# A linear-attention and mixture-of-experts kernel on one core: the first ten steps of the pipeline in a written-out order

## The chip, the cores and the metric

The kernel runs on one core of a Trainium2 chip. The metric is the device time of one execution, in microseconds (us). A core has five instruction streams that run side by side [...]: PE (TensorE, the matrix multiplies; PEld is its weight load), ACT (ScalarE), DVE (VectorE), POOL (GpSimd) and SP (SyncE, which here issues nearly all loads). Each stream executes its own instructions strictly in the order in which the program lists them.

## What is computed

The first half is a gated linear attention over 4 batches, 8 heads, 768 tokens and a head width of 48:

```
f = sigmoid(f_logit)
for t in range(S):
    state = f[t, :, None] * state + outer(k[t], v[t])
    y[t]  = q[t] @ state
```

The second half sends each of the 3072 rows (384 wide: 8 heads by 48) to one of 8 experts. The reference is

```
logits = x @ w_gate;  e = argmax(logits);  gate = softmax(logits)[e]
out[row] = gate * (relu(x[row] @ w1[e]) @ w2[e])        # w1: 384 x 1024, w2: 1024 x 384
```

All of it is in 32-bit floats.

## The kernel before

**Units and steps.** The attention is cut into chunks of 128 tokens. One *unit* is one chunk of two batches, so there are 12 units (NU = 12), each of 8 head pairs, which stand as two *halves* `a` and `b` of four pairs. Units `u` and `u+2` follow each other in time for the same two batches; their state passes from one to the other. What one unit needs, with the function and the line (of the kernel before) that the profile shows, and the engine:

- `load` (SP, L485): f, k, q, v of a unit from memory, each into the next of 2 (f), 3 (k), 4 (q) or 3 (v) buffers.
- `steps` (ACT, L495) and `log` (ACT, L503): exp and ln of the gate; `total` (DVE, L510): the running sum of the logs; `growth` (ACT, L524): r = exp(sum); `decay` (ACT, L539): exp(-sum), over the gate's own buffer.
- `by_r` (POOL L528, for some units DVE L528): k times r, in place; `by_decay` (DVE, L551): q times the decay, in place. `ends` and `last_decay` (POOL, L534 and L546) copy the last column of the sum and of the decay.
- `score` (PE, L562): k against q into four PSUM banks; `mask` (DVE, L568): four predicated copies, half `a` first, into `at`.
- `keys` (PE, L577): the scaled k transposed; `keep` (ACT, L582): copied to `kn`.
- `within` (PE, L590): v against the masked scores into `yt`; `before` (PE, L611): the old state against q, added to `yt`; `settle` (ACT, L652): `yt` copied to `ys`.
- `added` (PE, L627): `kn` against v, the state's increment `dp`; `update` (DVE L642 for units 0 and 1, L644 later; then POOL, L646): new state.
- `rows` (PE, L682): `ys` times the gate matrix and a selection matrix, which brings the tokens onto partitions; then the logits' reduction (DVE, L690); `lay` (ACT, L707 and L712): the rows copied to `xr`.
- For each two units one `Route`: `choose` (DVE, L228 to L236), `count` (PE, L240 and L241), `weigh` (ACT, L268), `place` and `fill` (DVE, L247 to L274), and `send` (POOL, L195): indirect DMAs that put each row into its expert's region.

**PSUM.** Scores have four banks, `yt` has two (one tile for both halves), and the transposed keys, `dp` and the rows' result share the last two: `turns` gives these tiles in alternation to two banks, so each waits until the tile two before it has been read out.

**What sets the order.** The pool's scheduler is switched off (`manual_schedule`): each engine's stream is the order in which the Python code calls the functions. A first block (L716 to L822) handles the start: loads, 24 filler multiplies into `yt` (`warm`, L729), units 0 and 1 by halves, 8 more fillers. Then comes the loop `for n in range(1, NU + 2)`: step n scores unit n (`here`), works `within` and `before` on n-1 (`back`), makes the rows of n-2 (`last`), and runs the gates of n+1 to n+3 ahead. Cases for n of 1, 2 and 3 put the pieces of the first steps in other places of the step. From step 10 on no gates are left but a rest of unit 11's.

**After the loop** the eight experts are worked: `widen` (L336, two matrix products with a 1024-wide hidden layer, ReLU at L346 on ACT and L348 on DVE), `narrow` (L352, the result scaled at L363 on DVE and scattered at L195 on POOL), and for the rows that do not fit an expert's regular blocks the quads (L1121, L1147, L380). The first row blocks of experts 0 and 1 are begun in the loop's last steps (n of 12 and 13).

The functions that the change touches, as they were:

Of the kernel before, what the change touches and what calls it, by code (L numbers as in the profile page):

```python
# [19 lines left out]
C = 128  # L20
# [100 lines left out]
def kernel(  # L121
# [318 lines left out]

    with ExitStack() as st:
# [7 lines left out]
        yt = psy.tile([128, 2, HP, C], F32, name="yt")  # L449
        nc.vector.memset(yt, 0.0)  # L450
# [119 lines left out]
        def keys(u):  # L570
            x = units[u]
            x["kn"] = wk.tile([128, SEG, C], F32, name="kn", bufs=1)
            x["kp"] = []
            for a in range(2):
                kp = turns("kp", [128, HP, C])
                for p in range(HP):
                    nc.tensor.transpose(kp[:, p], x["k"][:, HP * a + p], ident)  # L577
                x["kp"].append(kp)

        def keep(u):  # L580
            for a in range(2):
                nc.scalar.copy(units[u]["kn"][:, HP * a : HP * a + HP], units[u]["kp"][a])  # L582

        def within(u, a):

            x = units[u]
            if a == 0:
                x["yt"] = yt
            for p, h, _ in heads():
                nc.tensor.matmul(  # L590
                    x["yt"][DP * (h ^ a) : DP * (h ^ a) + D, a, p],
                    lhsT=x["v"][:, a, 2 * p + h],
                    rhs=x["at"][:, a, h, p],
                    start=p == 0,
                    stop=x["old"] is None,
                    skip_group_check=True,
                )

        def before(u):
# [6 lines left out]
            for p in range(HP):  # L606
                for h in range(2):
                    for a in range(2):
# [3 lines left out]
                            x["yt"][to : to + D, a, p],  # L612
# [7 lines left out]
        def added(u):  # L620
# [3 lines left out]
            for a in range(2):  # L624
                for p, h, r in heads():
# [3 lines left out]
                        lhsT=x["kn"][:, s, r],  # L629
# [6 lines left out]
        def update(u):  # L636
# [3 lines left out]
            last = _bc(x["last"], 2, D)  # L640
# [5 lines left out]
            return lambda: nc.gpsimd.tensor_tensor(new, new, last, op=OP.mult)  # L646

        def settle(u):
            x = units[u]
            x["ys"] = wk.tile([128, 2, HP, C], F32, name="ys", bufs=1)  # L650
            for a in range(2):
                nc.scalar.copy(x["ys"][:, a], x["yt"][:, a])  # L652
# [10 lines left out]
        def rows(u, counted=None):  # L663
# [11 lines left out]
            x["xr"], x["xp"] = group["xr"][:, 2 * (u - g[0]) :], []  # L675
            for a in range(2):
                j = 2 * (u - g[0]) + a
                xp, counts = pair()
                if a and counted:
                    counted.count(counts[:, :, 0 : counted.n])  # L680
                for p in range(HP):
                    done["rows"] = nc.tensor.matmul(  # L682
                        xp[:, p],
                        lhsT=x["ys"][:, a, p],
                        rhs=wx[:, p, 0:XW] if a else wx[:, p, E:WX],
                        start=True,
                        stop=True,
                    ).ins
                gate = slice(0, E) if a else slice(2 * D, XW)
                nc.vector.reduce_sum(  # L690
                    group["lg"][:, j],
                    xp[:, :, gate].rearrange("p h e -> p e h"),
                    axis=AX_X,
                )
                x["xp"].append(xp)
# [4 lines left out]
        def lay(u):  # L700

            x = units[u]
            for a in range(2):
                to = x["xr"][:, a, 0:DM].rearrange("p (h w) -> p h w", h=HP)
                if a:
                    for h in range(2):
                        nc.scalar.copy(  # L707
                            to[:, :, D * h : D * h + D],
                            x["xp"][a][:, :, XW - D * h - D : XW - D * h],
                        )  # L710
                else:
                    nc.scalar.copy(to, x["xp"][a][:, :, 0 : 2 * D])  # L712
# [4 lines left out]
        load(0, "f", ab)  # L717
        load(0, "k")
        load(1, "f", ab[:1])
        load(0, "q")  # L720
        load(1, "f", ab[1:])
        load_first_consts()
        load(1, "kq")
        for i in (1, 0):
            nc.gpsimd.memset(scores[i], 0.0)
        def warm(count):

            for _ in range(count):
                nc.tensor.matmul(yt[:, 0, 0], lhsT=pad[:, 0:C], rhs=pad[:, 0:C], start=True, stop=True)  # L729

        warm(24)
        for part in ab:
            steps(0, part)
            total(0, part)
        load(2, "f")
        load(0, "v")
        for part in ab:
            growth(0, part)
            by_r(0, part, nc.vector)
            decay(0, part)  # L740
        for part in ab:
            by_decay(0, part)
        ends(0)
        last_decay(0)
        lay_selection()
        for part in ab:
            steps(1, part)
        load(3, "f")
        load(2, "k")
        load(1, "v")  # L750
        load(2, "q")
        load_gate()
# [42 lines left out]
        score(0, 0)  # L795
        score(0, 1)
        keys(0)
        warm(8)
        for part in ab:
            total(1, part)  # L800
        for a, part in enumerate(ab):
            growth(1, part)
            by_r(1, part)
            decay(1, part)
            for h in range(2):
                mask(0, a, h)
            scaled = by_decay(1, part)
            if a == 0:
                routed.append(scaled)
        ends(1)  # L810
        last_decay(1)
        steps(2)
        load(4, "f")
        load(3, "k")
        load(3, "q")
        load(2, "v")
        total(2)
        keep(0)
        steps(3, logs=False)
        growth(2)  # L820
        load(5, "f")
        load_consts()  # L822

        for n in range(1, NU + 2):
            here, back, last = n, n - 1, n - 2
            ahead = n + 1 < NU
            state = n < NU - 2
# [3 lines left out]
            if 2 < last:  # L831
                settle(last)
# [5 lines left out]
            if ahead and not 1 < n < 4:  # L838
# [11 lines left out]
            if n == 1:  # L850
                units[0]["old"] = None
                added(0)
                update(0)()
            if ahead and not 1 < n < 4:
                decay(n + 1)
                last_decay(n + 1)
            if state:
                keys(here)
                keep(here)
            if 1 < n < 4:  # L860
                growth(n + 1)
                if n == 3:
                    by_r(n + 1)
                ends(n + 1)
                decay(n + 1)
                last_decay(n + 1)
            if here < NU:
                for a in range(2):
                    for h in range(2):
                        if n == 2 and a and h:  # L870
                            by_r(n + 1, on=nc.vector)
                        mask(here, a, h)
            if n == 1:
                log(3)
                within(0, 0)
                within(0, 1)
                settle(0)
            if n == 1:
                steps(4, logs=False)
# [488 lines left out]
```

## Time and profile before

| | us |
|---|---|
| runs of the kernel before | 389.91, 390.06, 401.82; median 390.06 |
| the profiled execution's own time | 393.27 |
| span of its instructions, first to last | 391.5 |
| PE / DVE / ACT / POOL busy in the span | 377.9 / 171.0 / 102.8 / 113.7 |
| granted TensorE clock, mean | 0.996 |
| first score starts | 9.94 |
| scores of units 1 to 11 start | 15.04, 23.88, 32.26, 41.95, 52.48, 61.95, 71.33, 80.57, 89.95, 99.16, 106.46 |
| first multiply of the experts (L336) | 119.47 |

The span lies inside the time of the execution, 393.27 - 391.5 = 1.8 us around it. "Busy" counts each engine by itself, so the shares do not add up. PE's ends are modelled: two neighbouring groups of multiplies overlap by some 0.07 us in the list, and a group that holds a short wait shows as a longer group. In the list in order of time a row is: start, duration, engine, line, operation, output and inputs, count, and in brackets the idle time before it and what ended it. A 32-bit multiply stands as two entries (x16 is eight multiplies).

### The profile page before, as it was taken

What the parts mean: (1) busy time and instruction counts of PE and PEld (TensorE: products, weight loads), DVE (VectorE), ACT (ScalarE), POOL (GpSimd) and SP (SyncE); (2) the same over time, 40 slices, a digit from 0 to 9 for tenths busy, and PEclk for the clock granted to TensorE, in tenths of its full rate; (3) what the DMA queues carried; (4) which work ended last, traced back from release to release, by engine and by line L of the source; (5) the groups of instructions that cost most, each with busy time, mean ns of one, the idle gap of its engine ahead of it and who ended that gap; (6) DMA issues with size and microseconds to landing.
All of it is one profiled execution on the core that took longest, in us unless ns stands there. A gap on an engine that the chain in (4) does not pass through costs nothing.

```text
span 391.5 us, 7712 instructions
## 1 busy us (share of the span) xinstructions
PE 377.9 (97%) x3054; PEld 264.7 (68%) x3054; DVE 171.0 (44%) x366; ACT 102.8 (26%) x190; POOL 113.7 (29%) x120
## 2 busy tenths in 40 slices
PE   7899999999999999999999999999999999999993
PEld 7887888999989678685555555654466466464452
DVE  6998998979663632112121131116413013111450
ACT  7887977775432001010100110000010010001000
POOL 5772688897645310100001001000100100100011
PEclk9999999999999999999999999999999999999998
DMA  7999657778982359694549999898173469992231
GB/s 276 384 396 359 206 200 256 233 223 315 395 295 106 127 157 321 166 322 101 191 123 397 237 399 395 201 401 236 40 260 94 101 233 387 404 407 95 80 122 42
DMA packets 51659, 94.81 MB, mean 242 GB/s; under 512 B 20840, under 2 KB 40875, under 8 KB 49568
## 3 DMA queue, kind: packets, MB, share of 16 engines
q1 hardware_dynamic: 48448, 84.62, 64.0%
q0 software_dynamic: 3168, 9.64, 6.6%
q8 instruction: 25, 0.41, 0.4%
q14 instruction: 18, 0.15, 0.1%
HBM read 79.23 MB, written 15.21 MB: 241 GB/s over the span
## 4 chain that ended last, share of the span: by engine, by line
PE 84%; DVE 8%; issue 2%; DMA 2%; ACT 1%; POOL 1%; SPq 0%; POOLq 0%; DVEq 0%; ACTq 0%
PE hps L336 28%; PE yps L352 24%; PE yps L1147 7%; PE xp L682 5%; PE yt L590 4%; PE s L562 4%; PE s L336 3%; DVE sum L510 3%; PE hps L1121 3%; PE yt L611 2%; PE yp L352 2%; DVE at L568 2%; DMA q<-in_qu_dram 2%; DVE q L551 1%; PE kp L577 1%
## 5 line engine op out<-in xcount | busy, mean ns | idle before, releaser
L336 PE MATMUL hps<-xT,w1t 128*128 128x352 f32 (+2 forms) x384 | 110.1, 447 | 0.0
L336 PEld LDWEIGHTS hps<-xT,w1t 128*128 128x128 f32 x384 | 72.7, 190 | 37.2 <-issue 1.9
L352 PE MATMUL yps<-w2t,hT 128*128 128x384 f32 x288 | 94.4, 487 | 0.0
L195 POOL DMA_INDIRECT out_dram<-ysb,dst x24 | 23.4, 975 | 224.4 <-DVE ysb L363 214.7
L352 PEld LDWEIGHTS yps<-w2t,hT 128*128 128x128 f32 x288 | 54.6, 190 | 38.6 <-issue 1.5
L346 ACT ACTIVATE hT<-hps 128x352 f32<-128x352 f32 (+2 forms) x28 | 13.8, 491 | 200.4 <-PE hps L336 171.7
L348 DVE TENSOR_SCALAR hT<-hps 128x352 f32<-128x352 f32 (+2 forms) x28 | 15.6, 558 | 93.0 <-PE hps L336 93.0
L363 DVE TENSOR_SCALAR ysb<-yps,tg 128x384 f32<-128x384 f32 x22 | 13.6, 618 | 74.4 <-PE yps L352 55.6
L195 POOL DMA_INDIRECT xs<-xr,posi x24 | 32.9, 1371 | 18.7 <-issue 4.3
L568 DVE COPY_PREDICATED at<-mpack,s 128x512 f32<-128x512 uint8 x48 | 31.3, 727 | 4.9 <-PE s L562 4.9
L510 DVE TENSOR_TENSOR_SCAN sum<-g,cap 128x1032 f32<-128x1032 f32 (+1 forms) x14 | 28.9, 2070 | 2.6 <-ACT g L503 2.6
L528 POOL TENSOR_TENSOR k<-k,r 128x1024 f32<-128x1024 f32 (+1 forms) x11 | 24.1, 2190 | 14.1 <-ACT r L524 7.1
L1147 PE MATMUL yps<-qw,hqT 128*32 128x192 f32 (+1 forms) x192 | 27.5, 381 | 0.3 <-issue 0.2
L562 PE MATMUL s<-q,k 64*128 64x128 f32 x384 | 24.9, 279 | 1.8 <-POOL rend L534 1.3
L682 PE MATMUL xp<-wx,ys 128*128 128x104 f32 x192 | 25.2, 281 | 0.9 <-ACT kn L582 0.7
L562 PEld LDWEIGHTS s<-q,k 64*128 64x128 f32 x384 | 22.5, 188 | 3.9 <-issue 1.9
L590 PE MATMUL yt<-at,v 128*48 128x128 f32 x384 | 25.1, 276 | 0.0
L682 PEld LDWEIGHTS xp<-wx,ys 128*128 128x128 f32 x192 | 22.7, 191 | 2.8 <-issue 1.4
L590 PEld LDWEIGHTS yt<-at,v 128*48 128x48 f32 x384 | 20.0, 123 | 2.6 <-issue 1.5
L1147 PE MATMUL yps<-w2t,hT 128*32 128x384 f32 x192 | 21.4, 487 | 0.0
L551 DVE TENSOR_TENSOR q<-q,g 128x1024 f32<-128x1024 f32 (+1 forms) x14 | 16.5, 1188 | 0.3 <-DMA q<-in_qu_dram 0.3
L1147 PEld LDWEIGHTS yps<-w2t,hT 128*32 128x32 f32 x192 | 7.6, 110 | 13.0 <-issue 12.5
(116 smaller groups left out, 362.5 us busy)
## 6 DMA issues: line engine op xcount, KB each, us to landing
qw<-in_moe_w_dram SPq DMA_DIRECT2D x16, 1536.0 KB
w1t<-in_moe_w_dram SPq DMA_DIRECT2D x8, 1536.0 KB
w2t<-in_moe_w_dram SPq DMA_DIRECT2D x8, 1536.0 KB
k<-in_ku_dram SPq DMA_DIRECT2D x12, 512.0 KB
q<-in_qu_dram SPq DMA_DIRECT2D x12, 512.0 KB
f<-in_fu_dram SPq DMA_DIRECT2D x10, 512.0 KB
xs<-pad SPq DMA_DIRECT2D x8, 600.0 KB
v<-in_vu_dram SPq DMA_DIRECT2D x12, 384.0 KB
```

The source lines that it names most:

```text
L195: ins = nc.gpsimd.indirect_dma_start(out=dst, out_offset=bass.IndirectOffsetOnAxis(ap=idx, axis=0), in_=src, in_offset=None, bounds_check= ...
L336: nc.tensor.matmul(x["h"][:, f], lhsT=w[0][:, j, b * 128 : b * 128 + 128], rhs=x["xT"][:, j], start=j == 0, stop=j == KD - 1,)
L348: nc.vector.tensor_scalar(to, x["h"], 0.0, None, op0=OP.max)
L352: nc.tensor.matmul(yp, lhsT=x["hT"][:, f, t * C : t * C + C], rhs=w[1][:, f, :], start=f == 0, stop=f == NF - 1,)
L510: nc.vector.tensor_tensor_scan(x["sum"][:, part].rearrange("p s c -> p (s c)"), x["g"][:, part].rearrange("p s c -> p (s c)"), cap[:, part ...
L528: ins = on.tensor_tensor(k, k, units[u]["r"][:, part], op=OP.mult).ins
L551: return nc.vector.tensor_tensor(q, q, x["dec"][:, part], op=OP.mult).ins
L562: done["score"] = nc.tensor.matmul(ps[h][:, p], lhsT=x["k"][r, s], rhs=x["q"][r, s], start=True, stop=True).ins
L568: nc.vector.copy_predicated(x["at"][:, a, h], _bc(causal, 1, HP), x["ps", a][h])
L590: nc.tensor.matmul(x["yt"][DP * (h ^ a) : DP * (h ^ a) + D, a, p], lhsT=x["v"][:, a, 2 * p + h], rhs=x["at"][:, a, h, p], start=p == 0, st ...
L682: done["rows"] = nc.tensor.matmul(xp[:, p], lhsT=x["ys"][:, a, p], rhs=wx[:, p, 0:XW] if a else wx[:, p, E:WX], start=True, stop=True,).ins
L1147: nc.tensor.matmul(yp[r], lhsT=h[:, f, at : at + T], rhs=w[:, f, cols], start=f == 0, stop=f == NF - 1, skip_group_check=True,)
```

## The change

The code before and at the start of the loop, up to and including step 9, is replaced by one string, FIRST_STEPS, of short pieces. `lf0a` is "load f of unit 0, half a", `sc3b` "score of unit 3, half b", `kp` the transposed keys, `keep` their copy, `wi` within, `bef` before, `dp` added, `upd` and `updp` the two parts of update, `set` settle, `xp` and `lg` and `lay` the rows, their logits and their copy, `mx` and `my` the masks of a half, `exp ln sum r dec` the gates, `kr krx krv` by_r (plain; behind the latest DVE result named; on DVE), `q` by_decay, `oh ex place send` the route, `fill` the fillers. A regular expression reads the string and calls the functions one after the other; since the schedule is manual, each engine's stream is the string's order, filtered. The loop now runs from step 10 to 13 and keeps the order it had for these steps.

Three tiles are split by halves, so that a half can be written while the other is still in use: `kn` (two tiles, one buffer each), `ys` (two tiles) and `yt` (two PSUM tiles of one bank each). Counted on each engine, the instructions are the same before and after by kind and number (PE 1663, ACT 239, POOL 189, SP 467), except that DVE's zeroing of `yt` is two instructions instead of one (454 for 453). SP's stream of loads is the same, load for load.

```diff
+    FIRST = 10
+    FIRST_STEPS = """
+        lf0a exp0a ln0a fill24 lf0b exp0b lk0 ln0b sum0a dec0a sum0b ends0 lf1a lq0 lf1b r0a
+        r0b exp1a krv0a krv0b consts0 kp0a lk1 ln1a q0a sc0a lq1 exp1b ln1b dec0b keep0a
+        sum1a sel0 fill8 dec1a r1a sum1b r1b kr1a q0b q1a kp0b kr1b keep0b lf2 lv0 lf3 lk2
+        lv1 mx0a my0a lq2 sc0b mx0b my0b last0 dp0 upd0 sc1a exp2 ln2 wi0a gate0 lf4 kp1a
+        dec1b lk3 lq3 lv2 kp1b ends1 sum2 ends2 q1b exp3 lf5 wi0b set0a keep1a last1 mx1a
+        sc1b my1a mx1b r2 krx2 consts1 keep1b dp1 my1b wi1a set0b kp2a upd1 kp2b dec2 q2 ln3
+        sum3 ends3 exp4 ln4 upd0p upd1p sc2a mx2a sc2b keep2a keep2b my2a last2 dec3 line0
+        r3 xp0a xp0b set1a lq4 wi1b last3 lg0a lay0a mx2b my2b set1b wi2a wi2b dp2 lg0b krv3
+        bef2 line1 line2 lk4 lv3 lf6 pads0 lk5 lv4 lay0b kp3a exp5 ln5 sum4 r4 q3 exp6 sc3a
+        sc3b upd2 krx4 upd2p kp3b mx3a my3a keep3a xp1a dec4 mx3b my3b keep3b xp1b lg1a q4
+        lg1b last4 lay1a dp3 sum5 lq5 lay1b sc4a sc4b ends4 ends5 oh1 kp4a upd3 lf7 set2a
+        wi3a set2b wi3b mx4a my4a mx4b ln6 kp4b lk6 r5 kr5 dec5 q5 keep4a xp2a lv5 keep4b
+        bef3 exp7 lg2a xp2b lay2a set3a set3b dp4 lq6 lf8 lk7 sum6 sc5a lg2b lay2b my4b
+        ends6 dec6 upd4 ex1 place1 ln7 wi4a q6 sc5b lv6 r6 upd3p kp5a kp5b lq7 last5 last6
+        mx5a kr6 lf9 wi4b lk8 lv7 keep5a line3 xp3a keep5b xp3b my5a sc6a mx5b upd4p my5b
+        sc6b lg3a exp8 ln8 lay3a lg3b lay3b bef4 oh3 lq8 set4a lf10 set4b send5 sum7 r7 krx7
+        dec7 last7 dp5 kp6a sum8 upd5 wi5a ends7 ends8 mx6a my6a mx6b wi5b bef5 kp6b line4
+        lk9 keep6a xp4a keep6b q7 my6b set5a lv8 lq9 ex3 xp4b dec8 lg4a lg4b lay4a sc7a q8
+        wi6a lay4b r8 place3 send6 dp6 upd6 kp7a sc7b mx7a my7a mx7b set5b line5 wi6b keep7a
+        kp7b xp5a my7b krx8 sc8a exp9 ln9 keep7b xp5b exp10 ln10 lg5a sum9 lg5b oh5 lay5a
...
+        bef8 my9a mx9b lg7a lay7a dp9 sum11 r11 lg7b lay7b my9b oh7 upd9
+    """
...
-        yt = psy.tile([128, 2, HP, C], F32, name="yt")
-        nc.vector.memset(yt, 0.0)
+        yt = [psy.tile([128, HP, C], F32, name=f"yt{a}") for a in range(2)]
+        for y in yt:
+            nc.vector.memset(y, 0.0)
...
-            x["kn"] = wk.tile([128, SEG, C], F32, name="kn", bufs=1)
...
+        def keys(u, a):
+            x = units[u]
+            x["kn", a] = wk.tile([128, HP, C], F32, name=f"kn{a}", bufs=1)
+            kp = x["kp", a] = turns("kp", [128, HP, C])
...
-            x["ys"] = wk.tile([128, 2, HP, C], F32, name="ys", bufs=1)
-            for a in range(2):
-                nc.scalar.copy(x["ys"][:, a], x["yt"][:, a])
+            for a in halves:
+                x["ys", a] = wk.tile([128, HP, C], F32, name=f"ys{a}", bufs=1)
+                nc.scalar.copy(x["ys", a], x["yt"][a])
...
+        for what, u, part in re.findall(r"([a-z]+)(\d+)([abp]?)", FIRST_STEPS):
+            DO[what](int(u), part)
...
-        for n in range(1, NU + 2):
+        for n in range(FIRST, NU + 2):
```

## The prediction

> **What bounds the kernel now.** I read the page's first part and its chain first: PE is busy 97% of the span and carries 84% of the chain, so an engine other than PE can only matter where PE stands still. Where that is, the page does not say; the busy times by stretch do. The columns are PE, PEld, DVE, ACT and POOL busy, then granted clock, DMA share, GB/s; the first score starts at 9.94.
>
> ```profile
> 9.94:20.00 10.06, 9.00 (x125) 8.14 (x126) 9.86 (x12) 8.65 (x16) 7.13 (x6) 1.00 1.04 381
> 20.00:30.00 10.00, 9.42 (x142) 8.58 (x143) 9.93 (x12) 8.02 (x13) 7.68 (x8) 1.00 1.02 400
> 30.00:40.00 10.00, 9.21 (x140) 8.08 (x140) 8.18 (x13) 7.98 (x16) 3.23 (x4) 1.00 0.87 328
> 40.00:50.00 10.00, 9.33 (x158) 8.39 (x154) 9.86 (x17) 9.12 (x15) 6.18 (x6) 1.00 0.59 200
> 50.00:60.00 10.00, 9.75 (x170) 8.48 (x166) 9.79 (x19) 7.88 (x16) 8.14 (x8) 1.00 0.59 198
> 60.00:72.00 12.00, 12.00 (x226) 10.70 (x224) 9.89 (x26) 8.80 (x16) 9.12 (x11) 1.00 0.83 266
> ```
>
> From 60 on PE has no idle time (39.20 of 39.20 us up to 99.2). Before that its gaps sum to 3.35 us, beside a DVE that is nearly full in four of five stretches. The chain of waits agrees: to 59.6 it runs over DVE, ACT and POOL, from there over PE alone. One undisturbed step of it gives PE's prices (start, us, what):
>
> ```profile
> 62.02 1.99 PE s L562 x32
> 64.00 1.02 PE kp L577 x8
> 65.03 1.01 PE yt L590 x16
> 66.04 1.07 PE xp L682 x8
> 67.11 0.16 PE xp L240 x2
> 67.27 0.22 PE xp L241 x2
> 67.49 0.95 PE xp L682 x8
> 68.45 1.01 PE yt L590 x16
> 69.46 0.92 PE dp L627 x32
> 70.38 1.02 PE yt L611 x32
> ```
>
> So a unit costs PE: score 1.99, keys 1.02, within 2.02, rows 1.96 (0.38 more in every second unit for the counts), dp 0.92, before 1.02: 9.1 us. The bound to any gain follows. By 59.60 PE has done 6 scores (11.94), 6 keys (6.12), 5 within (10.1), 4 rows with one count (8.2), 5 dp (4.6), 2 before (2.0) and the eight late fillers (1.95): 44.9 us of work in 49.66. Lost: 4.7, of which 3.3 are visible gaps and the rest waits inside groups. The same sum from 59.60 to 99.23 is 38.4 of 39.6: lost 1.2. With the fillers, 7.8 us could be had at the very most, which is just 2% of the time. What follows step 9 isn't touched, and starts as much earlier as PE gets there.
>
> **The change part by part.** *Nothing is removed or added* but one DVE zeroing split in two at the start (0.91 us before in one; the fillers wait 2.1 us on DVE's zeroing either way): 0 on the path, bounded by -0.1 and +0.1. The order of SP's loads is the same; f, k and q of units 0 and 1 wait for nothing computed, so q0 lands at 9.19 as before. Later loads wait for a buffer's last reader: k3 for unit 0's score, which I put 2 to 3 us later below, but f4 ahead of it on SP issues at 16.28 only because exp2 ends then, so k3 keeps its place; behind it lie q3, v2, f5, the second constants, q4, k4, all likewise. The DMA engines are full until 36 either way, and no load is waited for after q0: 0, with +1 if one comes late.
>
> *The order.* I followed each engine's new order by hand: an instruction starts when its engine is free and its inputs are there, at this trace's durations (ACT half 0.54, whole 0.96, exp whole 1.2; DVE half scan 1.27, scan 2.3, mask 0.65, q 0.6 a half and 1.2 whole; POOL half k 1.4, whole 2.37). Unit 0 loses: keys 0a now stand ahead of score 0a, and need the identity, whose arrival ends POOL's wait at 10.25, so score 0a is 10.75 to 11.75 (9.94 before); the fillers run to 13.7; keys 0b, score 0b 14.2 to 15.2; dp0 to 16.1. Score 1a then has what it needs (q1a 13.6, k1a 14.7): 16.1 to 17.1. Before, at 17.1, PE had 4.1 us of work done (fillers aside); after, 4.9. Behind it PE always has a piece whose inputs are there: within 0a, keys 1, within 0b to 20.1, score 1b, and dp1 at 21.5 (its copied key 1b ends then, 0.4 lost), within 1a; keys 2 wait for k2 on POOL (r2 20.95 + 2.37 = 23.4, 0.4 lost); q2 ends at 24.3, and score 2 starts at 24.4.
>
> Next, score 2 to 26.5; rows 0 wait for the bank of keys 2a (copied 26.85, 0.35 lost); within 1b to 29.9; within 2a for settle 1a, which ACT has behind dec3 and r3 (29.9). dp2, before 2, keys 3a to 34.3, when q3 is just done (sum3 26.7, masks, k3 on DVE 30.8, sum4 33.1, q3 34.3). Score 3, keys 3b, rows 1, dp3 to 39.7; q4 39.3; score 4 39.7 to 41.7. Unit 5's score starts at 49.2, unit 7's first half at 66.5, its second ends at 70.9 (before, score 7 starts at 71.39 in the chain). On the way PE ends keys 4a at 42.4, within 3 44.4, keys 4b 44.9, rows 2a 45.9, before 3 46.9, rows 2b 48.3, dp4 49.2, score 5a 50.2, within 4a 51.2, score 5b 52.2, keys 5 53.2, within 4b 54.2, rows 3 56.2, score 6 58.2, before 4 59.2, dp5 60.1, keys 6a 60.6, within 5 62.6, before 5 63.6, keys 6b 64.1, rows 4 66.5, score 7a 67.5, within 6a 68.5, dp6 69.4, keys 7a 69.9. It waits for none of them, since DVE ends q5 at 46.4, the last mask of unit 4 at 49.7, q6 53.0, the last mask of unit 5 at 55.6, unit 5's update 62.6, q7 65.8, and POOL ends k5 at 45.6, k6 55.3, k7 63.7. A check by work done:
>
> | at (after / before) | done after | done before | ahead |
> |---|---|---|---|
> | 24.4 / 23.88 | 11.9 | 9.9 | 2.0 - 0.5 = 1.5 |
> | 41.7 / 41.95 | 28.7 | 26.7 | 2.0 + 0.3 = 2.3 |
> | 53.2 / 52.48 | 40.0 | 36.0 | 4.0 - 0.7 = 3.3 |
> | 70.9 / 71.39 | 57.7 | 54.2 | 3.5 + 0.5 = 4.0 |
>
> The lead comes in two places: PE has keys and within of a unit to do while POOL and DVE finish the next k and q (20 to 34), and rows 2 no longer stand in a gap behind the copied keys (0.67 at 46.7).
>
> *The halves.* Split `kn`, `ys`, `yt` take waits off: within 2a needs settle 1a only. That lies inside the walk. What the walk leaves out is the handoff. The rows of before show it where an input is only just ready:
>
> ```profile
> 35.45 0.66 PE L577 MATMUL kp<-fpack,k 128*128 128x128 f32 x4 [0.55 <-DVE state L644]
> 31.19 1.14 PE L627 MATMUL dp<-v,kn 128*64 128x48 f32 x32 [0.25 <-ACT xr L712]
> 50.40 1.14 PE L627 MATMUL dp<-v,kn 128*64 128x48 f32 x32 [0.19 <-ACT xr L712]
> ```
>
> I take 0.2 for each of the walk's four short waits up to unit 2, about 0.7 in all: 4.0 - 0.7 = 3.3. From both sides: a gain of 4.0 and 0.5 of what is lost after unit 7, or 1.6 less than 3.3 if in eight steps one more bank is handed over late by 0.2.
>
> *The port.* One rule speaks against a tight order: the Trainium skill, "SBUF — State Buffer", section "Who interferes with whom", says that a VectorE instruction with two SBUF inputs and a GpSimd one that reads SBUF exclude each other for the whole instruction. The trace shows the price: q of unit 4 starts at 39.22 during POOL's k (37.76 to 40.13) and takes 1.99 instead of 1.21. The walk has such meetings at q1a (k1 of POOL at 13.35) and q5 (k5 43.2 to 45.6). By the row 0.8 each, by the rule up to 1.4 and 2.4. q1a would end at 15.0 instead of 13.6, under dp0 (to 16.1); q5 at 46.9 instead of 46.4 or, by the rule, 48.8, under before 3, rows 2b and dp4 (to 49.2). Both hide; without that cover they cost 1.6 by the row and 3.8 by the rule. I take 0.
>
> **Sum.** 391.5 - 3.3 = 388.2 of span; with the 1.8 us around it 390.0, against 393.27 for the profiled run. The median of the runs is 390.06, 3.2 below that run, so the time is 390.06 - 3.3 = 386.8.
>
> **The rivals.** *Most of the lead is lost to handoffs.* PE's waits of 0.2 to 0.5 come back at every bank of the two that keys, dp and rows share, now three to five times a step in a new order. Lead 0.5 to 2: 388.0 to 389.6, say 389. For it: DVE at 9.8 of 10 us leaves little for the early copies that free these banks. Against it: from 60 to 106 the same rotation runs without a gap.
>
> *PE is dense from the first score on.* 4.7 + 1.2 lost come back, less 1.3 at the start: gain 4.6 to 6, 384.5. Against it: the walk itself already shows 1.3 us of waits.
>
> *DVE becomes the bound (slower).* Place: units 3 to 9. DVE's step is sum 2.3, q 1.2, masks 2.6, state 0.54, logits 0.35, half a route 1.45: 8.45 against PE's 9.1. If POOL's k, sum ends and last-decay copies meet sum and q in each step, at 0.8 for each of two, a step is 10.05, 0.9 over PE's: seven steps cost 6.3, 386.8 + 6.3 = 393. It decides from 0.7 us of meetings a step, and the gain is gone at 1.2. For it: DVE's 9.86 of 10 between 40 and 50. Against it: 8.1 to 8.4 a step between 60 and 99 with the same work, and POOL's k stand behind a named DVE result in units 2, 4, 7 and 8.
>
> *It does nothing:* the stages before 60 would have to be hidden, but the chain runs straight through them.
>
> **How the numbers follow.** As forecast (gain 2.2 to 4.5, 385.6 to 387.9): 0.58. Handoffs (388 to 389.6): 0.20. Dense (384 to 385.5): 0.11. DVE bound or a late load (390 to 398): 0.11. The range of 8 in 10 leaves a tenth at each end: 384.5 to 390.0. 2%, which is about what a measurement of this kernel can tell from no change, is 7.8 us, all that PE's losses hold: faster by more 0.03; slower by more (over 397.9, DVE at 1.9 us of meetings a step) 0.03; within 0.94.
>
> **What would show it.** Score 0 starting near 10.7, later than before; PE's idle time from there to 60 at about 1.3 instead of 3.35; score 7's second half over at 70.9; the experts' first multiply at 116.2 instead of 119.47; the expert part itself unchanged in length (272.0 from there). Wrong if PE's gaps recur after 60, where DVE would then be full, or if a load is named as a releaser after q0.

## The result, and the profile after

The changed kernel takes 388.42 us (median of 22 runs, 387.05 to 390.20), the kernel before 390.04 beside it; the ratio is 0.9966, 95% interval 0.9954 to 0.9978, a gain of 1.3 us by the ratio (1.6 by the medians) where 3.3 was forecast. Its runs lie in two groups with 0.63 us between them: 13 from 387.05 to 388.60 (middle one 387.70), 9 from 389.23 to 390.20 (middle one 389.79), the latter at a mean granted clock of 0.991 to 0.995 (0.9926 on average), the former at 0.995 to 0.999 (0.9974). Two slow runs of the kernel before, 401.82 and one read as 999.0, stay out of the ratio; its other 20, from 388.96 to 390.68, are one group. The profiled execution took 388.52, its span is 386.5.

The same stretches as in the prediction, now of the kernel after (PE, PEld, DVE, ACT, POOL busy, granted clock, DMA share, GB/s):

```profile
9.94:20.00 10.06, 8.97 (x126) 8.07 (x127) 9.35 (x11) 8.87 (x17) 4.36 (x6) 1.00 1.04 382
20.00:30.00 10.00, 9.92 (x149) 8.80 (x148) 9.60 (x14) 9.72 (x15) 5.25 (x10) 1.00 1.01 365
30.00:40.00 10.00, 9.98 (x186) 9.18 (x183) 9.22 (x14) 8.46 (x15) 3.73 (x7) 1.00 0.93 357
40.00:50.00 10.00, 10.00 (x176) 9.03 (x172) 9.86 (x17) 8.28 (x17) 3.17 (x4) 1.00 0.76 255
50.00:60.00 10.00, 10.00 (x154) 8.96 (x152) 8.46 (x25) 7.13 (x13) 6.13 (x7) 1.00 0.63 235
60.00:72.00 12.00, 12.00 (x215) 10.81 (x208) 11.21 (x23) 8.61 (x16) 8.11 (x9) 1.00 0.70 241
```

The gaps are gone: from 20 to 60 PE stands still for 0.1 us instead of 2.29 (the missing 1.09 of the first row is the time before the first piece, at 11.03). The list of PE's waits up to the experts has four entries left (what waited, for what, us in total, times, longest):

```profile
PE yt L754 <- DVE yt L482: 1.6, 1, 1.6
PE kp L607 <- DMA fpack<-c_fpack: 1.4, 1, 1.4
PE xp L717 <- ACT ys L681: 0.2, 1, 0.2
PE s L337 <- DVE xT L320: 0.2, 1, 0.2
```

The last one was not there before: the experts' first multiply waits for `xT`, the transposed rows. The chain of waits of the kernel after (start, us, what) runs through the rows at that place, where PE carried it alone in the forecast:

```profile
101.98 0.78 POOL state L673
102.77 0.17 issue
102.94 1.84 POOL xs L196
104.77 0.31 issue
105.08 5.77 DMA xs<-xr,posi
...
112.38 4.24 DMA xrow<-xs
...
116.75 0.71 DVE xT L320
117.45 0.04 issue
117.50 2.27 PE s L337 x18
```

The sixth pair of row scatters is issued at 102.94 and 105.08, its last packets land at 110.85, only then SP may read the first expert's rows back, the last of four reads lands at 116.62, DVE transposes, and PE starts at 117.50. In the profile of before PE reached this point at 119.47, and the pair and the first read were issued at:

```profile
102.14 1.04 POOL L195 DMA_INDIRECT xs<-xr,posi  x1 [0.15 <-issue]
103.49 1.40 POOL L195 DMA_INDIRECT xs<-xr,posi  x1 [0.30 <-issue]
...
110.03 1.89 SPq L289 DMA_DIRECT2D xrow<-xs  x4
```

So PE came 2.0 us earlier, the second scatter 1.6 and the read 1.0 later. Over more profiles the second scatter goes out at 103.17 to 103.49 in the old order (four of them) and at 104.10 to 105.08 in the new one (seven, with the sixth pair in this place). And the rows travel while the DMA engines are still full (last two columns: DMA share, GB/s), after:

```profile
110.00:112.00 2.00, 1.82 (x39) 1.50 (x38) 0.83 (x7) 1.21 (x4) 0.56 (x1) 1.00 1.07 386
112.00:114.00 2.00, 2.00 (x20) 1.90 (x22) 1.36 (x9) 0.77 (x2) 1.65 (x4) 1.00 1.03 365
114.00:116.00 2.00, 2.00 (x44) 1.81 (x44) 1.06 (x7) 0.76 (x3) 0.00 (x0) 1.00 0.79 244
```

In before the share falls from 1.10 to 0.85 at 112 already.

How long PE took from its first real piece to the experts' first multiply, in seven profiles and, last, one of a slower chip (the wait for the rows is taken off in the last column):

| kernel | first piece | experts start | wait for rows | between |
|---|---|---|---|---|
| before, the profile of the prediction | 9.94 | 119.47 | 0 | 109.5 |
| before_gap (below) | 10.30 | 118.97 | 0 | 108.7 |
| split_alone (below) | 10.15 | 118.86 | 0 | 108.7 |
| before_reads2 (below) | 10.22 | 118.88 | 0 | 108.7 |
| after | 11.03 | 117.50 | 0.16 | 106.3 |
| fill_more (below) | 10.33 | 118.18 | 1.60 | 106.3 |
| sends_shift (below) | 10.75 | 116.89 | 0 | 106.1 |
| after_same (below, on a slower chip) | 10.12 | 117.45 | 0 | 107.3 |

The order is worth 2.4 us (108.7 less 106.3). The profile that the prediction read is 0.8 longer than the other three of the old order: three of its groups `yt<-q,state` took 1.35 to 1.40 instead of 1.09. Against this profile `after_same` is 2.2 shorter.

### The profile page after: what moved, and what is told of

It is laid out like the page before. It is cut to its first block, busy times and chain, and to the rows that moved or that the text cites. A ratio compares the mean times of both kernels' runs of the same rounds, so it can differ in the third digit from the quotient of the medians.

```text
span 386.5 us, 7693 instructions
## 1 busy us (share of the span) xinstructions
PE 377.2 (98%) x3054; PEld 264.6 (68%) x3054; DVE 170.2 (44%) x367; ACT 102.3 (26%) x190; POOL 98.9 (26%) x120
## 4 chain that ended last, share of the span: by engine, by line
PE 85%; DMA 6%; issue 2%; POOL 2%; DVE 1%; SPq 1%; ACT 1%; POOLq 0%; ACTq 0%; DVEq 0%
PE hps L337 28%; PE yps L353 24%; PE yps L1143 7%; PE s L594 5%; PE yt L618 4%; PE xp L717 3%; DMA xs<-xr,posi 3%; PE s L337 3%; PE hps L1117 3%; PE yp L353 3%; PE kp L607 2%; DMA fpack<-c_fpack 2%; PE dp L655 2%; PE yt L639 1%; DMA xrow<-xs 1%
## 5 line engine op out<-in xcount | busy, mean ns | idle before, releaser
L600 DVE COPY_PREDICATED at<-mpack,s 128x512 f32<-128x512 uint8 x48 | 32.1, 732 | 3.1 <-PE s L594 3.1
L560 POOL TENSOR_TENSOR k<-k,r 128x1024 f32<-128x1024 f32 (+1 forms) x11 | 25.2, 2296 | 20.5 <-ACT r L556 14.6
L196 POOL DMA_INDIRECT xs<-xr,posi x24 | 25.5, 1063 | 13.7 <-issue 4.6
L594 PE MATMUL s<-q,k 64*128 64x128 f32 x384 | 26.3, 281 | 0.1
L618 PE MATMUL yt<-at,v 128*48 128x128 f32 x384 | 24.3, 276 | 0.0
```

Source lines behind the costliest of these rows:

```text
L196: ins = nc.gpsimd.indirect_dma_start(out=dst, out_offset=bass.IndirectOffsetOnAxis(ap=idx, axis=0), in_=src, in_offset=None, bounds_check= ...
L560: ins = on.tensor_tensor(k, k, units[u]["r"][:, part], op=OP.mult).ins
L594: done["score"] = nc.tensor.matmul(ps[h][:, p], lhsT=x["k"][r, s], rhs=x["q"][r, s], start=True, stop=True).ins
L600: nc.vector.copy_predicated(x["at"][:, a, h], _bc(causal, 1, HP), x["ps", a][h])
L618: nc.tensor.matmul(x["yt"][a][DP * (h ^ a) : DP * (h ^ a) + D, p], lhsT=x["v"][:, a, 2 * p + h], rhs=x["at"][:, a, h, p], start=p == 0, st ...
```

## The experiments

Ratios are to the kernel before on the same chip, with 95% intervals. The chips differ: on two of the five used for experiments the kernel before takes 392.4 to 392.5, on the other three 389.8. The profile of before in the prediction, 393.27, is like those of the first two: in it, as in four other profiles from such chips (`after_same`, `sends_shift2`, `sends_early`, `before_late`), PE waits twice more behind the experts' start (0.4 to 0.5 for "issue", 0.3 for `hT`).

**Theory and rivals.** Theory: the lead is there but runs into the rows of the sixth scatter, and PE's wait for them brings a drop of the clock in part of the executions. Rivals: the clock drops for the gap at the start (1.40 us ahead of the first keys); the half pieces cost what the gaps cost; the split of tiles does the work, not the order.

**The split and the order apart.** `order_alone` keeps the written order and makes `kn`, `ys`, `yt` one tile each:

```diff
-        yt = [psy.tile([128, HP, C], F32, name=f"yt{a}") for a in range(2)]
+        yts = psy.tile([128, 2, HP, C], F32, name="yt")
+        yt = [yts[:, a] for a in range(2)]
...
-            x["kn", a] = wk.tile([128, HP, C], F32, name=f"kn{a}", bufs=1)
+            x["kn", a] = x["kn"][:, HP * a : HP * a + HP]
...
-                x["ys", a] = wk.tile([128, HP, C], F32, name=f"ys{a}", bufs=1)
+                x["ys", a] = x["ys"][:, a]
```

> The changed kernel with its written-out order, but with copied k, settled y and y's banks each in one tile as before. Theory: the order carries the gain, and the split removes only waits of a tenth or two: 388.4 to 389.2. Rival (the split is what lets the halves overlap): 390 or more.

Measured: 401.88, ratio 1.0229 (1.0189 to 1.0269), 9 us slower. PE's waits in its profile:

```profile
PE yt L620 <- ACT ys L685: 2.2, 3, 0.8
...
PE xp L721 <- ACT kn L612: 1.9, 2, 1.7
PE s L594 <- DVE q L583: 1.4, 1, 1.4
PE dp L657 <- ACT kn L612: 0.8, 1, 0.8
```

A half that may not be written until the other half has been copied stops PE again and again, and behind the wait of 1.7 the granted clock is at 0.50 for 6.83 us. `split_alone` is the kernel before with the three tiles split as in the change, and nothing else.

> The kernel before with kn, ys and yt in tiles by halves, in the order before. Theory (the split only allows the order, which is what moves the time): ratio 0.998 to 1.001, first expert multiply within 0.5 of 119.5. Rival (the split itself gives what was gained): ratio 0.995 to 0.998, with fewer waits of PE for ACT's copies before 60.

Measured: 389.87, ratio 1.0000 (0.9992 to 1.0008). The split is nothing by itself and the condition of the order.

**The start.** `before_gap` is the kernel before with fewer fillers, `fill_more` the change with more, which closes the gap ahead of the first keys.

```diff
-        warm(24)
+        warm(18)
...
-        lf0a exp0a ln0a fill24 lf0b
+        lf0a exp0a ln0a fill29 lf0b
```

> The kernel before with 18 early fillers instead of 24, which opens a gap of some 1.5 us ahead of its first score. Theory (clock): a second cluster of runs about 2 us longer, with lower mean clocks, appears in the kernel before too; its shorter cluster stays at the kernel before's time. Rival: the time stays at 1.000 within 0.001 with one cluster, as PE only waits for q there.

> The changed kernel with 29 early fillers instead of 24, so that PE stays busy over the 1.4 us in which it waits for the identity ahead of keys 0a. Theory (clock: that gap lets the granted clock fall to half in some executions, which are the runs about 2 us longer with a mean clock of 0.991 to 0.995): the longer cluster vanishes, no run has a mean clock under 0.995, and the ratio to the kernel before goes from 0.9966 to about 0.994. Rival (the spread comes from the rows' scatter and read ahead of the experts, or from loads): two clusters stay and the ratio stays at 0.9966 within 0.001, or grows by the fillers' 0.1 to 0.3 us.

Measured: `before_gap` 390.05, 1.0004 (0.9996 to 1.0013), one group, a gap of 2.05 us at the start and the full clock behind it: the rival of the start falls. `fill_more` 388.42, 0.9959 (0.9947 to 0.9970), no gap at the start, and still 2 of 17 runs at 390.48 and 390.68 (9 of 22 for the change, which did not run on this chip). The profile is of the latter run (list in order of time, then stretches with PE's columns and the clock):

```profile
116.21 0.37 PE L242 MATMUL rp<-oh,fpack 128*128 128x16 f32 x2
118.18 3.63 PE L337 MATMUL s<-xT,w1t 128*128 128x128 f32 x18 [1.60 <-DVE xT L320]
121.59 2.25 PE L717 MATMUL xp<-wx,ys 128*128 128x104 f32 x16
```

```profile
115.44:118.84 3.40, 1.80 (x34) 1.52 (x25) 1.30 (x7) 1.07 (x2) 1.57 (x2) 1.00 0.39 102
118.84:122.25 3.41, 3.41 (x19) 3.41 (x18) 0.71 (x5) 0.00 (x0) 1.86 (x3) 0.50 0.29 112
122.25:125.60 3.35, 3.35 (x31) 3.35 (x31) 1.44 (x9) 1.37 (x5) 2.67 (x5) 1.00 0.39 151
```

PE waits 1.60 us for the rows, and right after it the granted clock is 0.50 for 3.41 us: the 18 entries of the experts' first group take 3.63 instead of 2.25. The wait costs itself and another 1.7 (half of 3.41). The scatter is not late here: its second part goes out at 104.32, 0.8 us earlier than in the profile after, but it takes 7.02 us to land and the read behind it 4.41, instead of 5.77 and 4.24. So whether an execution is hit depends on the DMAs as well as on POOL's order.

`score_first` moves the first keys behind the first score, as before; `ident_early` loads the identity behind k of unit 0:

```diff
-        r0b exp1a krv0a krv0b consts0 kp0a lk1 ln1a q0a sc0a lq1
+        r0b exp1a krv0a krv0b consts0 lk1 ln1a q0a sc0a kp0a lq1
```

```diff
-        ... exp0b lk0 ln0b sum0a ... krv0b consts0 kp0a
+        ... exp0b lk0 consts0 ln0b sum0a ... krv0b kp0a
```

> The changed kernel with keys 0a behind score 0a, so that PE's first work waits for q0 and not for the identity. Theory (clock and start): the gap is 0.4 to 0.9 us instead of 1.4, fewer dips, first score near 10.1, keys 0a right behind it: ratio 0.994 to 0.995. Rival: 0.9966 within 0.001.

> The changed kernel with the identity and the mask loaded ahead of f 1a and q 0 instead of behind them. Theory (clock and start): keys 0a no longer wait for the identity, they start at about 9.7 and score 0a right after q0 (10.1); the gap ahead of the first work falls under 0.8 us, clock dips vanish, and the first score is about 1 us earlier: ratio about 0.993. Rival (start hidden by later waits): the first score is earlier but the ratio stays at 0.9966 within 0.001.

Measured: 387.45, 0.9932 (0.9918 to 0.9947), and 387.77, 0.9943 (0.9930 to 0.9956), each in one group, of no more than 6 and 5 runs. With no scatter moved they gain 2.7 and 2.2 us by their ratios. In both PE meets the rows (waits of 0.57 and 0.90 us), and the clock stays at 1.00; first keys at 8.46 instead of 11.03 move the experts' start only from 117.50 to 117.29.

**The scatters.** Four edits moved them. `sends_early` moved the third to fifth (the sixth stayed in the loop); `sends_late` and `before_late` put seven memsets of 128 by 256 on POOL ahead of the sixth, in the new and in the old order.

```diff
-        ... my7b krx8 sc8a ... sum10 kr9 mx8a ... send7 r10 kr10 sc9b send8 ... xp7b send9
+        ... my7b krx8 send7 sc8a ... sum10 kr9 send8 mx8a ... r10 kr10 send9 sc9b ... xp7b
...
+            if n == 10:
+                for _ in range(7):
+                    nc.gpsimd.memset(idle, 0.0)
             scatter_some("score" if n == NU - 1 else None)
```

> The changed kernel with three of its row scatters (send7, send8, send9) put further forward in POOL's stream, behind k of units 8, 9 and 10, so that the sixth scatter, which the experts' first row read waits for, leaves POOL some 4 us sooner. Theory (the scatter, the read of its rows and their transpose end no sooner than PE is ready, so PE's lead over the kernel before is partly waited away): the experts' first multiply no longer waits for the transposed rows, the median falls to about 387.2, and the runs above 389 vanish. Rival (the lead was never larger than 1.6 us, since the late first score and the cuts between half pieces took it): the median stays at 388.4 within 0.4, with the same spread.

> The changed kernel with seven small POOL fills (some 2 us in all) put ahead of the sixth row scatter. Theory: the chain from that scatter to the experts' first multiply sets the end, so the time rises by nearly all of it, 1.5 to 2.0 us, to about 390.2. Rival: the chain has slack, and the time stays at 388.4 within 0.4.

> The kernel before with the same seven POOL fills (some 2 us) ahead of its sixth row scatter. Theory: here PE reaches the experts 2 us later while the scatter leaves 1.6 us sooner, so some 3 us of slack cover it: 390.0 within 0.4. Rival (the chain sets the end in both kernels): 391.5 to 392.

Measured: `sends_early` 390.84, 0.9972 (0.9955 to 0.9989): the sixth stayed at 102.89 and PE got a new wait of 1.2 us for DVE's state, so the edit did not test what it was made for; 3 of its 14 runs are long (392.69 to 393.81, clock 0.991 to 0.994). `sends_late` 391.84, 0.9996 (0.9977 to 1.0014): the sixth at 105.84, experts at 118.48, all of the gain spent, but not on the rows. They are transposed by 118.0 and no wait of PE names them; PE waits 1.87 us for `hT`, the experts' hidden layer, at 126.3 instead. `before_late` 393.20, 1.0022 (1.0012 to 1.0032), 0.9 slower where nothing was expected: the experts start at 120.36 there, again with no wait for rows. So the memsets cost something else, and the pair speaks neither for the theory nor against it.

In `sends_shift` the third pair goes into POOL's idle time (75.35 to 81.30 in the profile after), and the fourth to sixth take the places of the third to fifth. `shift_ident` and `shift_score` add the two edits of the start.

```diff
-        ... upd5p last8 upd6p set6a ...
+        ... upd5p last8 upd6p send7 set6a ...
...
-        ... xp7a xp7b send9
+        ... xp7a xp7b send10
```

> Written order; the third pair of row scatters goes into POOL's idle time before the k of unit 9, and the fourth, fifth and sixth take the places of the third, fourth and fifth, so that step 10 has none left. Same instructions. Theory (the last row scatter, its landing and the row read cap PE's lead at the experts' start): the sixth scatter runs near 97 to 99 instead of 103 to 106, the row reads start near 105 to 107 instead of 111, PE's first expert multiply no longer waits for the transposed rows, the granted clock falls nowhere, and the runs no longer fall into two groups: ratio to before 0.991 to 0.994 with all runs near the short group. Rival (the lead is lost in the half pieces or at the start, the row wait is a symptom): the wait goes, but the time stays at 0.9955 to 0.998.

> The scatters pulled forward as in sends_shift and, as well, the identity loaded behind k of unit 0, ahead of f of unit 1 and q of unit 0. Theory: two independent gains that add up once the cap is gone; first keys near 8.5, first score near 10, first expert multiply near 116.3 (117.3 with the late rows), ratio 0.988 to 0.992. Rival (what caps the start of the experts is another chain, for instance weights or DVE): first expert multiply at 117 or later, ratio as without the scatters' move, 0.993 to 0.9955.

> The scatters pulled forward as in sends_shift and, as well, the first keys behind the first score, as before. Theory: first score near 10.3, first expert multiply near 116.6 instead of 117.2, no wait for the rows, ratio 0.989 to 0.993. Rival (another chain caps the start of the experts): 117 or later, ratio 0.9925 to 0.995.

Measured: 387.31, 0.9938 (0.9925 to 0.9951), five runs from 387.00 to 387.60; 387.02, 0.9933 (0.9920 to 0.9946), 386.85 to 387.50; 387.63, 0.9951 (0.9937 to 0.9965), one of six at 388.74 and clock 0.992. The chain of `sends_shift` at the place that was the rows':

```profile
109.79 1.09 PE yt L639 x32
...
111.56 2.03 PE xp L717 x16
113.59 1.88 PE yt L618 x32
115.47 1.02 PE yt L639 x32
116.49 0.32 PE rp L241 x2
116.82 0.22 PE rp L242 x2
117.04 2.10 PE s L337 x18
```

PE alone, no wait. The rows are not as much earlier as their scatter: it goes out 6 us earlier, the reads start at 108.15 instead of 111.05, and `xT` is transposed from 115.50 instead of 116.75, after the DMA share has fallen (0.79 from 112 on). The starts' edits bring the experts to 116.41 and 116.16, as expected, but of these 0.5 to 0.7 us no more than 0.3 shows in the time, and in `shift_score` nothing: that part is inside the intervals.

That was another chip than the changed kernel's own, so three kernels ran side by side on one. `after_same` is the change as it is; `sends_shift2` is `sends_shift`; `sixth_back` leaves the sixth pair in step 10 (`send7` added as in `sends_shift`, `send9` left out, nothing in its place).

> The changed kernel as it is, beside the next two on one chip. Theory (the sixth row scatter, and the drop of the clock that PE's wait for it brings in part of the executions): ratio 0.995 to 0.998, runs in two groups about 2 us apart, the longer one at a mean clock lower by about 0.004. Rival (the two groups belong to the chip of the first measurement): one group, and a ratio like that of the kernel with the scatters moved.

> The same kernel as sends_shift, on the chip of after_same. Theory: ratio 0.992 to 0.995, one group, 0.5 to 1.5 us under the median of after_same. Rival: equal to after_same within its interval.

> As sends_shift, but the sixth scatter is left in step 10, where the change has it: the third goes into POOL's idle time, the fourth and fifth move up one place. Theory: the sixth scatter at 100 to 103, still behind k of unit 11 but about 2 us earlier for POOL's free slot ahead of it; the row reads start near 108 to 110, PE waits 0 to 0.5 us for the transposed rows; between after_same and sends_shift2, ratio 0.993 to 0.996. Rival (any of the other scatters is what held PE up): equal to sends_shift2 with its sixth scatter late.

Measured: 389.91, 0.9935 (0.9916 to 0.9955); 390.30, 0.9937 (0.9919 to 0.9955); 389.38, 0.9928 (0.9901 to 0.9955), with two of seven runs at 392.41 and 392.54. On this chip (before: 392.5) the theory's difference is not there: the change has one group (of six runs) and the full 2.6 us, which is what the rival said, that the two groups belong to the chip of the first measurement. On a chip that shows two groups, the change and the moved scatters never ran side by side. The profile of `after_same` shows no loss at that place: the scatter goes out at about the same time (102.61), but the DMA share falls to 0.73 at 112 already, not at 114, the rows are there when DVE comes to transpose them at 115.76, and PE, at 117.45, finds them done. Of the two long runs of `sixth_back` one was profiled, and it has another wait: 1.88 us of PE for `hT` of the first expert at 125.1, and a clock of 0.56 from 126.4 to 129.8. So the same change gives 1.3 us on one chip and 2.6 on another; that the difference comes from this alone, which of the two comes first at the experts, PE or the rows, is argued from one profile of each.

**The wait by itself.** In the kernel before nothing waits for the rows. Three kernels delay only the row reads, by 8, 12 and 16 small reads of the same rows ahead of them on SP:

```diff
+                few = wk.tile([128, 3, 4, 16], F32, name="few", bufs=1)
+                for d in range(3):
+                    early_reads.extend(
+                        nc.sync.dma_start(
+                            few[BK * j : BK * j + BK, d],
+                            xs[first[0] : first[0] + C, 0:16].rearrange("(i c) m -> c i m", c=BK),
+                        ).ins
+                        for j in range(4)
+                    )
                 soon = [load_rows(first[e]) for e in range(EARLY)]
```

> The kernel before, with eight small reads of the same rows (32 partitions by 4 by 16 numbers each) issued by SP ahead of the two row reads of the first experts, some 0.43 us each; nothing else changes. The row reads start near 113.3 instead of 110, the rows are transposed near 119 to 121, PE waits 0.5 to 2 us for them. Theory (a wait of about 1.6 us or more within one 3.4 us stretch halves the clock for the next 3.4): the wait alone in most executions, ratio 1.001 to 1.005, some 1.7 us longer ones among them if the wait passes 1.6. Rival (the wait costs only itself): one group, extra time equal to the wait in the profile.

> As before_reads2 with twelve small reads: row reads near 115, wait 2.2 to 3.7 us. Theory: extra time of the wait plus 1.7 us in most executions, ratio 1.009 to 1.014, mean clock lower by 0.004. Rival: extra time equal to the wait, ratio 1.005 to 1.009, clock as before.

> As before_reads2 with sixteen small reads: row reads near 116.8, wait 4 to 5.5 us. Theory: extra time of the wait plus 1.7 to 3.4 us in all executions, ratio 1.014 to 1.022. Rival: the wait alone, ratio 1.010 to 1.014.

| | row reads start | wait of PE in the profile | time | ratio |
|---|---|---|---|---|
| before_reads2 | 114.04 | 0 | 389.62 | 0.9998 (0.9989 to 1.0007) |
| before_reads3 | 116.33 | 2.82 | 394.66 | 1.0134 (1.0076 to 1.0192) |
| before_reads4 | 117.61 | 4.15 | 396.46 | 1.0177 (1.0158 to 1.0197) |

Reads 4 us later cost nothing (a wait of 0.5 to 2 was expected): issued when the DMA engines are no longer full, they take less to land, and DVE ends the transposition at 118.8, just when PE comes (118.88). Reads 6 us later cost 4.9. Stretches of `before_reads3`:

```profile
117.00:120.40 3.40, 1.85 (x42) 1.38 (x38) 0.00 (x0) 1.07 (x3) 0.98 (x1) 0.96 0.33 64
120.40:121.60 1.20, 0.00 (x0) 0.00 (x0) 0.68 (x3) 0.00 (x0) 0.97 (x1) 0.50 0.71 207
...
122.40:125.80 3.40, 3.40 (x18) 3.40 (x17) 0.65 (x5) 0.00 (x0) 1.53 (x2) 0.50 0.35 117
125.80:127.00 1.20, 1.20 (x8) 1.20 (x7) 0.00 (x0) 0.00 (x0) 0.90 (x2) 0.52 0.37 143
```

The clock is halved while PE still waits, and for 5.3 us after it has begun to multiply again at 121.67. `before_reads2` has eight of the same twelve reads, no wait and no stretch with a lowered clock, so the wait brings the drop: of 4.9 us, 2.8 are the wait and 2.1 what comes with it; of 6.7 in `before_reads4`, 4.1 and 2.5 (medians of four runs each, with the wait of one profile each). Not every execution is hit: one of the four runs of `before_reads3`, 392.84 at clock 0.995, is only 3.0 us over, about the wait alone.

## Why the prediction was wrong

**What bounds the kernel: right.** PE had 3.3 us of visible gaps up to 60; the order removed all but 0.1 of those from 20 on, with no load behind q0 as a releaser and no gap that recurs after 60.

**The walk: near in its times, wrong in its waits and in one price.** It ended unit 7's second half at 70.9 for a first piece at 10.25, 60.65 behind it; the profile after (11.03) has it end at 72.3, `after_same` (10.12) at 71.3, `sends_shift` (10.75) at 72.0, each 61.2 behind it. The late half microsecond is a balance. The 1.3 us of waits that the walk left PE up to 60 do not show (0.1 in the list), nor do the 0.7 put on for handoffs; but the pieces cost more than their price, above all half a score, which the walk put at half a whole one ("score 5a 50.2", from 49.2). The list in order of time of the kernel after:

```profile
49.96 1.16 PE L594 MATMUL s<-q,k 64*128 64x128 f32 x16
51.05 1.08 PE L618 MATMUL yt<-at,v 128*48 128x128 f32 x16
52.06 1.16 PE L594 MATMUL s<-q,k 64*128 64x128 f32 x16
53.15 1.09 PE L607 MATMUL kp<-fpack,k 128*128 128x128 f32 x8
54.17 1.08 PE L618 MATMUL yt<-at,v 128*48 128x128 f32 x16
```

From start to start half a score is 1.09 and a whole one 1.99. The new order has six units' scores in halves, the old one had one: 5 times 0.19 is 1.0 us more of PE's time. PE's busy time from first piece to experts (`split_alone`, then `fill_more`; the second number behind the window) agrees:

```profile
10.15:118.86 108.71, 105.13 (x1705) 94.84 (x1705) 94.04 (x193) 77.37 (x139) 75.00 (x73) 1.00 0.82 294
10.33:118.18 107.85, 106.00 (x1707) 95.17 (x1705) 92.97 (x194) 77.46 (x141) 61.26 (x75) 1.00 0.81 294
```

The same multiplies keep PE busy for 0.9 more, while 3.3 of idle time go (3.6 in the old order, 0.3 left in the new one without the wait for the rows): some 2.4 remain. That the 0.9 is the half scores, with small gains and losses of other cuts that cancel, is a sum and not a test. The row of before that showed it, 1.16 for half of score 1, was there to be read. Beside the profile that the prediction read the gain looks like 3.2 (109.5 less 106.3), but 0.8 of that is in the three long groups of that execution, which the other three profiles of the old order in the table do not have: two errors cancel, and the near hit would be luck.

**The start: right on average, late in the profile.** A first piece at 10.25 was forecast; eight profiles with this start have it between 10.04 and 11.03, because the identity lands at a different time in each. The profile after is the latest of them. The old order, whose first score waits for q, starts at 9.94 to 10.30.

**"What follows step 9 isn't touched, and starts as much earlier as PE gets there": this step failed.** It holds only for PE's own work. The experts' first multiply has a second condition, the rows of the sixth scatter, which POOL issues behind k of unit 11; in the new order POOL idles from 75.35 to 81.30, does the third, fourth and fifth pair between k of units 9 and 11, and the second scatter of the sixth, which the read waits for, 0.6 to 1.9 us later than before. The experts were forecast at 116.2; they start at 117.50 after a wait of 0.16 in the profile after, at 118.18 after 1.60 in that of `fill_more`. A wait in that place costs its length and, in the profiles with one of 1.60 us and more, a drop of the clock. So of the 3.3 that were forecast, 0.9 went to the half pieces, and of the 2.4 left a further 1.1 was lost on average behind step 9. The 13 short runs of the changed kernel are 2.1 us under the kernel before by their mean, the 9 long ones 0.1, and together they make the 1.3 of the ratio.

What of this is shown and what is argued: that a wait for the rows alone halves the clock is shown (`before_reads3` and `before_reads4`), and that it does so in a long run of the new order is shown in `fill_more`. No long run of the changed kernel itself was profiled; that its second group is this wait is argued from its clock, lower by 0.005 on average (3.4 us at half of 386 us give 0.0044), from the second group's absence in all ten runs of `sends_shift` and `shift_ident`, and from its absence where the rows come early (`after_same`). Ten runs are few: at the rate of `fill_more`, 2 long ones in 17, ten would show none in three cases of ten (an estimate from that rate). And the chip itself stays as a rival, since `after_same` has no second group in its six runs, with no scatter moved. Why a wait of 0.57 to 0.90 left the clock at 1.00 in the profiles of `score_first` and `ident_early`, and where exactly it begins, stays open. So does the single long run of `shift_score`.

**The port, the halves' handoffs, DVE: taken at 0 or little, and rightly.** No wait of PE in the list names them; DVE is fuller than before between 60 and 72 (11.21 of 12 us against 9.89), and PE still does not wait for it. (Of POOL's k 0.91 us was left when q of unit 4 began, so its 0.8 is nearly all that was left: by the row and by the rule are one price here, not two.) "Experts' part unchanged in length" holds: 269.0 us after, 268.8 to 269.2 in the three ordinary profiles of before; the 272.0 of the prediction's profile belong to that execution, and the 3.2 us between it and the median were rightly left out of the sum.

**The rivals.** Handoffs (389), dense (384.5), DVE (393) and nothing (390): 388.42 is nearest to the first, for another reason. The rival that was missing is the one that the word "earlier" calls for: what else does the next stage need, and when is that ready? The trace of before had it: the row reads start at 110.03, and with the 6.4 us that the profile after takes from there to the end of the transpose (111.05 to 117.46) the rows are there at about 116.4, an estimate, while the forecast had PE there at 116.2. There was nothing to spare for a later scatter or for DMA engines that stay full two microseconds longer.

## What to carry to other kernels

Before a lead on the busiest engine is carried into the next stage, follow that stage's first instruction back through every other input, here scatter, landing, read and transpose: the lead is worth at most the slack of the slowest of them, and an order that packs the other engines may have pushed that one later. Price a half piece by a row of a half piece, not by half of a whole. And where the time is in two groups, compare the mean clocks of the groups first.

## What the hardware showed

A wait of PE can cost more than its length. Waits of 1.60 (`fill_more`), 1.88 (`sixth_back`) and 4.15 us (`before_reads4`) went with half the granted clock for about 3.4 us, one of 2.82 (`before_reads3`) for 6.83, of which 5.3 lay behind the wait, and in `order_alone` a gap of 1.66, with 1.74 us of work in the 3.40 ahead of the drop, for 6.83. The Trainium skill, "TensorE: Matmul & The Clock Gate", section "HAM oscillation — how this bites in real kernels", names gaps of over 3.4 us as what to avoid; by that rule `fill_more`'s 1.60 and `before_reads3`'s 2.82 would have cost only themselves, and the measurement decides against it. Against a plain threshold of length stand `before_gap`, whose gap of 2.05 us in the first 11 us left the clock at 1.00, and two profiles with the same wait in the same place, the first of `sends_late`, the second of `sixth_back`:

```profile
128.18 5.43 PE L353 MATMUL yp<-w2t,hT 128*128 128x384 f32 x16 [1.87 <-ACT hT L347]
126.98 7.02 PE L353 MATMUL yp<-w2t,hT 128*128 128x384 f32 x16 [1.88 <-ACT hT L347]
```

In the first the clock stays at 1.00, in the second it is halved, and the same eight multiplies take 1.6 us longer. The same page, "Part 1: The HAM clock gate", says that the activity window runs freely and does not start with the kernel, which would explain why only a part of the executions is hit; no run here shows the phase.

With the DMA engines full, an indirect scatter of 128 rows took 5.8 us from its issue to its landing (105.08 to 110.85), and a read of 48 KB of the same rows 4.2; in `fill_more` they took 7.0 and 4.4. On another chip the engines emptied some 2 us sooner, the rows were transposed 1 us sooner, and the same kernel gained 2.6 us instead of 1.3. Whether loading the experts' weights (1.5 MB each, issued from 87.5 on in the new order, from 90.5 in the old) in another place would free the rows was not tried.
